# Half-swapped weight copies made on GpSimd in place of transfers, and a new order of the swap transfers

## The chip, the cores and the metric

The kernel runs on one core of a Trainium2 chip. Times are device microseconds of a whole execution, the median of several executions; the profile is one execution taken by the hardware profiler, and its span is some 2 us shorter than the time.

## The reference, cut to what matters

```python
# x: 2048 x 448;  H = 16 heads of 28;  F = 1792
q, k, v = split(x @ wqkv)
phi_q = concat(softmax(q @ w_phi), softmax(-(q @ w_phi)))     # per head
phi_k = concat(softmax(k @ w_phi), softmax(-(k @ w_phi)))
kv, z = phi_k^T @ v, sum over tokens of phi_k
a = (phi_q @ kv / (phi_q . z + 1e-6)) @ wo
b = gelu(x @ w1 + b1) @ w2 + b2
g = sigmoid((x * gate_w).sum(-1));   out = g * a + (1 - g) * b
```

## The kernel before: the parts that matter

The inner dimension 448 is 3.5 times 128. With x transposed in SBUF as `xT` (128 partitions, chunks 0 to 3, chunk 3 of use only in its upper 64 partitions), a plain product spends four matmuls on 3.5 chunks of work. The kernel therefore cuts 448 into seven pieces of 64 rows and lets the two 64-row halves of the array work at once, one for an even block of 512 tokens, one for the odd block after it. The array's lower half reads partitions 0 to 63 and its upper half 64 to 127, so each needs half of its pieces moved across by 64 partitions: `xS` holds those of x, `WqS`, `WkS`, `WvS` those of the weights.

```python
def x_half(i, k, h):                       # i: row half, k: piece 0..6, h: pair of blocks
    rows = slice(i * HP, (i + 1) * HP)     # HP = 64
    b = 2 * h + i
    if k == NK - 1:
        return xS[rows, 3, h, :] if i == 0 else xT[rows, 3, b * 512:(b + 1) * 512]
    if k % 2 == i:
        return xT[rows, k // 2, b * 512:(b + 1) * 512]
    return xS[rows, k // 2, h, :]

def swap_x(h):                             # ev, od: columns of the even and odd block of pair h
    nc.sync.dma_start(xS[0:HP, :, h, :], xT[HP:P, :, ev])          # "even half"
    nc.sync.dma_start(xS[HP:P, 0:3, h, :], xT[0:HP, 0:3, od])      # "odd half"

def load_x(b):                             # two transposing loads of block b from HBM
    nc.sync.dma_start_transpose(xT[:, 0:3, blk], x[blk, 0:384])    # "wide"
    nc.sync.dma_start_transpose(xT[:, 3, blk], x[blk, 320:448])    # "rest"

# ... earlier on the same queue: WkT, WqT, block 1
nc.gpsimd.dma_start(WvS[0:HP, 3, :], WvG[HP:P, 3, :])
nc.gpsimd.dma_start(x1o, xT[HP:P, 3, 512:1024])     # the "block 1 remainder"
load_x(2)
swap_w(WqS, Wpq)
swap_x(0)
load_x(3)
swap_w(WkS, Wpk)
swap_x(1)
swap_w(WvS, WvG, 3)
# ... w1, wo, w2

k_pair(0); k_pair(1); k_pair(2); k_pair(3)          # k of blocks 0 and 1: full-height matmuls
v_both()                                            # v of block 1: its last pieces paired, needs x1o, WvS
for g in range(4): q_pair(g, 0)                     # q of blocks 0, 1: needs xS pair 0, WqS
for r in range(4): k_two(r); v_two(r); q_pair(r, 1) # blocks 2, 3: need xS pair 1, WkS, WvS
# then 28 units of the dense layer, the kv sums, the output tiles
```

(The calls of `k_norm` between these, which normalize on VectorE and GpSimd, are cut.) All SyncE transfers go through one queue in this order.

The softmax here doesn't subtract the row's maximum and nothing guards it: scores larger than these inputs give would overflow.

## Time and profile before

| | before |
|---|---|
| time, median | 156.71 us (156.67 to 156.75) |
| span of the profiled execution | 154.7 us |
| TensorE busy | 149.5 us, 97% |
| its waits after the start | one, at 19.8 us, for `xS` |
| GpSimd busy | 34.1 us, 22% |
| DMA packets, bytes | 28306, 14.98 MB |

To read it: TensorE is nearly full, so what can be won is what it waits for; the DMA engines are full over the first third, and what they carry decides when TensorE may go on. The lines are in the prediction.

### The profile page before, as it was taken

Reading aid. Unit: us, or ns where it says so; the run is one execution under the profiler, and the core shown is the slowest. Engines: PE = TensorE matmul, PEld = TensorE weight load, DVE = VectorE, ACT = ScalarE, POOL = GpSimd, SP = SyncE. Lnnn points to the kernel's source line nnn. Section 1 sums busy time; section 2 is a strip of 40 time slices with the busy share of each in tenths; the row PEclk is TensorE's granted clock in tenths of the full one; section 3 lists DMA queues with packets and bytes.
Section 4 is the critical chain, followed back from the end, with each engine's and each line's share of the span. In section 5 each row is a group of like instructions: output and inputs, shape, how many; then the busy total and the mean of one; then the engine's idle time right before and its main releaser. Section 6 shows DMA issues by size and latency. Waiting matters only on the chain.

```text
span 154.7 us, 3189 instructions
## 1 busy us (share of the span) xinstructions
PE 149.5 (97%) x1302; PEld 81.2 (53%) x1302; DVE 83.1 (54%) x244; ACT 77.2 (50%) x93; POOL 34.1 (22%) x38
## 2 busy tenths in 40 slices
PE   7999979999999999999999999999999999999991
PEld 2775435555555854444444455555556555555561
DVE  3454989379892050000000059999977999977100
ACT  2569919999889626776767640111311111111121
POOL 7951596919876000000000000000000000000000
PEclk9999999999999999999999999999999999999999
DMA  4999999999993000000000001114332124338401
GB/s 150 229 232 154 209 233 254 221 222 215 218 356 130 4 0 4 0 0 4 0 0 0 4 0 34 34 38 96 92 96 64 40 64 92 82 82 39 121 31 30
DMA packets 28306, 14.98 MB, mean 97 GB/s; under 512 B 19938, under 2 KB 27876, under 8 KB 28292
## 3 DMA queue, kind: packets, MB, share of 16 engines
q1 hardware_dynamic: 27012, 14.00, 42.1%
q10 hardware_dynamic: 1152, 0.65, 1.5%
q0 software_dynamic: 128, 0.13, 0.7%
q8 instruction: 10, 0.16, 0.4%
q14 instruction: 4, 0.03, 0.1%
HBM read 6.11 MB, written 1.84 MB: 51 GB/s over the span
## 4 chain that ended last, share of the span: by engine, by line
PE 84%; SPq 9%; DMA 3%; issue 1%; DVE 0%; ACT 0%; ACTq 0%
PE hp L442 27%; PE y L501 27%; PE pq L320 8%; PE y L507 8%; PE nm L457 4%; PE v_ps L304 3%; PE pk L312 3%; DMA xS<-xT 3%; SPq L136 3%; PE acc L331 2%; SPq L132 2%; SPq L133 2%; SPq L384 1%; SPq L126 1%; SPq L141 0%
## 5 line engine op out<-in xcount | busy, mean ns | idle before, releaser
L501 PE MATMUL y<-w_sb,gel 128*128 128x448 bf16 (+2 forms) x238 | 45.2, 341 | 0.0
L442 PE MATMUL hp<-xT,w_sb 64*128 64x512 bf16 x196 | 42.3, 376 | 0.0
L442 PE MATMUL hp<-xS,w_sb 64*128 64x512 bf16 x196 | 41.9, 376 | 0.0
L447 ACT ACTIVATE gel<-hp,b1T 128x1024 bf16<-128x1024 f32 x28 | 30.8, 1110 | 13.0 <-PE hp L442 13.0
L510 ACT ACTIVATE res<-y,ungate 128x448 bf16<-128x448 f32 (+2 forms) x17 | 10.4, 611 | 50.3 <-PE y L507 50.2
L501 PEld LDWEIGHTS <-gel 128*128 128x128 bf16 x238 | 22.6, 98 | 19.6
L442 PEld LDWEIGHTS <-w_sb 64*128 64x128 bf16 x392 | 19.6, 94 | 22.5
L276 POOL TENSOR_TENSOR phik<-phik,rec 128x1792 bf16<-128x1792 bf16 (+1 forms) x8 | 24.9, 3126 | 9.8 <-DVE rec L273 9.8
L462 DVE COPY st<-nm 128x32 f32<-128x32 f32 x32 | 4.5, 184 | 35.5 <-PE nm L457 35.5
L478 DVE TENSOR_TENSOR tmp<-nm,al 128x448 bf16<-128x448 f32 x32 | 18.4, 617 | 0.0
L271 DVE TENSOR_REDUCE sums<-phik 128x64 f32<-128x1792 bf16 x8 | 16.0, 2000 | 2.8 <-ACT phik L264 2.8
L507 PE MATMUL y<-wo_sb,oT 128*128 128x448 bf16 (+2 forms) x68 | 14.7, 342 | 0.0
L320 PE MATMUL pq<-xT,Wpq 64*128 64x512 bf16 x56 | 13.0, 376 | 0.0
L320 PE MATMUL pq<-xS,WqS 64*128 64x512 bf16 x56 | 11.2, 376 | 0.9 <-DMA xS<-xT 0.9
L325 ACT ACTIVATE EqP<-pq 128x1024 bf16<-128x1024 f32 x8 | 8.4, 1051 | 5.1 <-PE pq L320 5.1
L193 DVE CAST vaug<-v_ps 128x896 bf16<-128x896 f32 x7 | 7.5, 1081 | 6.0 <-PE v_ps L304 3.3
L326 ACT ACTIVATE EqN<-pq 128x1024 bf16<-128x1024 f32 x8 | 8.4, 1055 | 0.0
L457 PE MATMUL nm<-KVbd,EqP 128*128 128x120 bf16 x64 | 8.3, 216 | 0.0
L457 PE MATMUL nm<-KVbd,EqN 128*128 128x120 bf16 x64 | 8.3, 216 | 0.0
L263 ACT ACTIVATE phik<-pk 128x896 bf16<-128x896 f32 x8 | 7.7, 961 | 0.3 <-PE pk L285 0.3
L507 PEld LDWEIGHTS <-oT 128*128 128x128 bf16 x68 | 6.0, 98 | 3.5
L264 ACT ACTIVATE phik<-pk 128x896 bf16<-128x896 f32 x8 | 7.8, 972 | 0.0
(99 smaller groups left out, 147.2 us busy)
## 6 DMA issues: line engine op xcount, KB each, us to landing
w_sb<-in_B_w_dram SPq DMA_DIRECT2D x4, 784.0 KB, 14.1
out_dram<-res SPq DMA_DIRECT2D x15, 112.0 KB, 1.9
w_sb<-in_B_w_dram SPq DMA_DIRECT2D x1, 1568.0 KB, 16.1
xS<-xT SPq DMA_DIRECT2D x2, 256.0 KB, 4.0
oT<-in_A_x_dram ACTq DMA_DIRECT2D x1, 448.0 KB, 3.2
xS<-xT SPq DMA_DIRECT2D x2, 192.0 KB, 4.3
WvS<-WvG SPq DMA_DIRECT2D x2, 168.4 KB, 3.9
wo_sb<-in_A_wo_dram SPq DMA_DIRECT2D x1, 336.0 KB, 17.1
```

The source lines that it names most:

```text
L271: nc.vector.reduce_sum(out=sums[:], in_=ph, axis=AX.X)
L276: eng.tensor_tensor(out=ph[:, lo:hi], in0=ph[:, lo:hi], in1=rec[:, lo:hi, :, None].to_broadcast([P, hi - lo, 2, DH]), op=ALU.mult)
L320: nc.tensor.matmul(pq[:, i, :], lhsT=w_half(Wpq, WqS, i, k)[:, g * P:(g + 1) * P], rhs=x_half(i, k, h), start=(k == 0), stop=(k == NK - 1))
L325: nc.scalar.activation(out=EqP[:, g, dst], in_=src, func=ACT.Exp)
L326: nc.scalar.activation(out=EqN[:, g, dst], in_=src, func=ACT.Exp, scale=-1.0)
L442: nc.tensor.matmul(hp[:, i, :], lhsT=w1_sb[i * HP:(i + 1) * HP, k, j * P:(j + 1) * P], rhs=x_half(i, k, h), start=(k == 0), stop=(k == NK ...
L447: nc.scalar.activation(out=gel[h][:, j, :], in_=hp[:].rearrange("p a b -> p (a b)"), func=ACT.Gelu_apprx_tanh, bias=b1T[:, j:j + 1])
L457: nc.tensor.matmul(nm[s][:, g * 2 * KW:(g + 1) * 2 * KW], lhsT=E[:, g, tok], rhs=KVbd[:, g, s, :], start=True, stop=True)
L478: nc.vector.tensor_tensor(out=tmp[:, s, :].rearrange("p (x h d) -> p x h d", x=NPR, h=2), in0=nmv[s][:, :, 0:PW].rearrange("p x (h d) -> p ...
L501: nc.tensor.matmul(y, lhsT=gel[t // 8][:, j, (t % 8) * P:(t % 8 + 1) * P], rhs=w2_sb[:, j, cols], start=(j == 0), stop=False)
L507: nc.tensor.matmul(y, lhsT=oT[:, c, tok], rhs=wo_sb[:, c, cols], start=False, stop=(c == NC4 - 1))
L510: nc.scalar.activation(out=res[:, cols], in_=y, func=ACT.Copy, scale=ungate[:, t:t + 1])
```

## The change

It has two parts. WkS, WvS and the block 1 remainder are made by GpSimd, which is almost idle between 9 and 17 us, by copies whose input and output are 64 partitions apart: 849 KB less for the DMA engines. And the first swap of x goes ahead of the loads of blocks 2 and 3.

```diff
-    nc.gpsimd.dma_start(WvS[0:HP, 3, :], WvG[HP:P, 3, :])
-    nc.gpsimd.dma_start(x1o, xT[HP:P, 3, 512:1024])
+    swap_on_pool(WvS, WvG)     # two nc.gpsimd.tensor_copy: [0:HP] <- [HP:P], [HP:P, 0:3] <- [0:HP, 0:3]
+    swap_on_pool(WkS, Wpk)
+    nc.gpsimd.tensor_copy(out=x1o, in_=xT[HP:P, 3, 512:1024])
+    swap_x(0, "even")
+    swap_w(WqS, Wpq)
+    swap_x(0, "odd")
     load_x(2)
-    swap_w(WqS, Wpq)
-    swap_x(0)
     load_x(3)
-    swap_w(WkS, Wpk)
     swap_x(1)
-    swap_w(WvS, WvG, 3)
```

The order of instructions on TensorE, VectorE and ScalarE stays as it was.

More of the change, by code (lines that the diff above doesn't have):

```diff
@@ L128, with load_x, swap_x @@
     nc.scalar.dma_start(wphi[:, 0:3, :], wphi_rows[0:384, :].rearrange("(c p) b -> p c b", p=P))
-    def load_x(b):
+    def load_x(b, part=None):
         blk = slice(b * 512, (b + 1) * 512)
-        nc.sync.dma_start_transpose(xT[:, 0:3, blk], x[blk, 0:384])
-        nc.sync.dma_start_transpose(xT[:, 3, blk], x[blk, 320:448])
+        if part != "rest":
+            nc.sync.dma_start_transpose(xT[:, 0:3, blk], x[blk, 0:384])
+        if part != "wide":
+            nc.sync.dma_start_transpose(xT[:, 3, blk], x[blk, 320:448])
     def load_wT(W, base):
         nc.sync.dma_start_transpose(W[:], A_wqkv[:, base:base + NC4 * P])
-    def swap_x(h):
+    def swap_x(h, part=None):
         ev = slice(2 * h * 512, 2 * h * 512 + 512)
         od = slice(2 * h * 512 + 512, 2 * h * 512 + 1024)
-        nc.sync.dma_start(xS[0:HP, :, h, :], xT[HP:P, :, ev])
-        nc.sync.dma_start(xS[HP:P, 0:3, h, :], xT[0:HP, 0:3, od])
+        if part != "odd":
+            nc.sync.dma_start(xS[0:HP, :, h, :], xT[HP:P, :, ev])
+        if part != "even":
+            nc.sync.dma_start(xS[HP:P, 0:3, h, :], xT[0:HP, 0:3, od])
     load_wT(WkT, D)
@@ L381, with swap_w, swap_on_pool @@
     prep(WqT, wq_at, (1, 0, 0))
-    def swap_w(W_S, W, chunks=NC4):
-        nc.sync.dma_start(W_S[0:HP, 0:chunks, :], W[HP:P, 0:chunks, :])
+    def swap_w(W_S, W):
+        nc.sync.dma_start(W_S[0:HP, :, :], W[HP:P, :, :])
         nc.sync.dma_start(W_S[HP:P, 0:3, :], W[0:HP, 0:3, :])
+    def swap_on_pool(W_S, W):
+        nc.gpsimd.tensor_copy(out=W_S[0:HP, :, :], in_=W[HP:P, :, :])
+        nc.gpsimd.tensor_copy(out=W_S[HP:P, 0:3, :], in_=W[0:HP, 0:3, :])
     nc.gpsimd.dma_start(b1c[0:NJ, :], B_b1.rearrange("(j p) -> j p", p=P))
     x1o = oT[0:HP, 1, 0:512]
-    nc.gpsimd.dma_start(WvS[0:HP, 3, :], WvG[HP:P, 3, :])
-    nc.gpsimd.dma_start(x1o, xT[HP:P, 3, 512:1024])
+    swap_on_pool(WvS, WvG)
[4 more added lines that the diff above has]
+    swap_x(0, "odd")
     load_x(2)
-    swap_w(WqS, Wpq)
-    swap_x(0)
     load_x(3)
-    swap_w(WkS, Wpk)
     swap_x(1)
-    swap_w(WvS, WvG, 3)
     for f in (slice(0, F // 2), slice(F // 2, F)):
```

## The prediction

> **What bounds the kernel now.** I read the page's busy table and slices first, to see which engine is full and where it is not.
>
> ```profile
> PE 149.5 (97%) x1302; PEld 81.2 (53%) x1302; DVE 83.1 (54%) x244; ACT 77.2 (50%) x93; POOL 34.1 (22%) x38
> ...
> PE   7999979999999999999999999999999999999991
> ...
> POOL 7951596919876000000000000000000000000000
> PEclk9999999999999999999999999999999999999999
> DMA  4999999999993000000000001114332124338401
> ```
>
> TensorE is busy for 97% of the 154.7 us span at full clock. One slice inside the run is not full: the sixth, 19.3 to 23.2 us. GpSimd (POOL) has a weak third slice (7.7 to 11.6 us) and an almost empty fourth (11.6 to 15.5 us), and the DMA engines are full from 4 us to about 46 us. So the question is what TensorE waits for in that slice. The waits of TensorE give it, the only wait of PE after its first instruction:
>
> ```profile
> PE pq L320 <- DMA xS<-xT: 0.9, 1, 0.9
> ```
>
> The timeline of TensorE (start, duration, line) shows it whole:
>
> ```profile
> 19.58 0.35 PE L220 MATMUL v_ps<-WvG,xT 64*128 64x449 bf16 x1
> 19.77 0.38 PE L320 MATMUL pq<-xT,Wpq 64*128 64x512 bf16 x1
> 21.03 0.39 PE L320 MATMUL pq<-xS,WqS 64*128 64x512 bf16 x2 [0.89 <-DMA xS<-xT]
> 21.24 0.39 PE L320 MATMUL pq<-xT,Wpq 64*128 64x512 bf16 x2
> ```
>
> The first query matmul of the lower 64 rows starts at 19.77. Its partner on the upper 64 rows would start 0.01 to 0.02 us later, as the pair at 19.57 and 19.58 did, but starts at 21.03: 1.24 us late. The 0.9 of the wait view is smaller because the earlier matmuls' modelled ends cover part. The chain that ended last says what it waits for and that nothing else follows:
>
> ```profile
> 16.40 4.59 DMA xS<-xT
> 20.99 0.04 issue
> 21.03 6.19 PE pq L320 x55
> 27.22 1.14 PE pk L312 x12
> ```
>
> From 21.03 to 151.5 us the chain is matmuls alone. So the change can give at most about 1.24 us here (one stagger of 0.2 us between the two row halves included), unless it breaks something else. The transfer in question is the second half of the swap of blocks 0 and 1 (L142), and the queue shows why it is late (start, duration of the issue):
>
> ```profile
> 8.97 1.26 SPq L133 DMA_TRANSPOSE xT<-in_A_x_dram  x1
> 10.27 1.71 SPq L132 DMA_TRANSPOSE xT<-in_A_x_dram  x1
> 12.03 1.26 SPq L133 DMA_TRANSPOSE xT<-in_A_x_dram  x1
> 13.47 0.56 SPq L383 DMA_DIRECT2D WqS<-Wpq  x1
> 14.08 1.52 SPq L384 DMA_DIRECT2D WqS<-Wpq  x1
> 15.64 0.65 SPq L141 DMA_DIRECT2D xS<-xT  x1
> 16.40 0.60 SPq L142 DMA_DIRECT2D xS<-xT  x1
> ```
>
> The transposes of block 2 (10.27 to 13.29), which nobody needs before the k matmuls at 26.87, stand ahead of it.
>
> **What the Trainium skill says.** "GPSIMD Engine Reference", section 4.1 (Engine selection), calls one-input operations on GpSimd roughly line-rate; section 3.1 puts light loops at 1.03 cycles an element and an ordinary tight loop at 1.8, at 1.2 GHz. The trace agrees with the first figure as far as it goes: the memset of 2048 elements took 1.80 us (0.88 ns each), the select rose from about 0.19 us for 4 elements to 0.29 us for 128 (0.8 ns each), and the two-input product of 1792 took 3.13 us (1.7 ns each, two reads). No large copy, and none between partitions, is in this trace. "SBUF — State Buffer", section "Who interferes with whom", says that VectorE instructions with two SBUF inputs, or in a 2-port mode, contend with GpSimd. The trace agrees: the half product at 46.32 us took 2.54 us instead of about 1.6 while VectorE ran the other half. Between 9.4 and 16.5 us VectorE does casts from fp32 PSUM (1.1 us for 896, one element a cycle) and a reduction, so I expect no such contention. "DMA: Bandwidth & Descriptors", section "Issuing engines are not separate DMA queues", says all queues share the same 16 engines; the trace agrees, DMA share 1.0 to 1.3 from 16 to 29 us at some 205 to 290 GB/s. So every byte taken out helps whatever stands behind it.
>
> **The change, part by part.**
> *Removed transfers.* WkS 224+168 KB, WvS 2x168.4 KB and 56 KB, x1o 64 KB: 849 KB. From the landing at 20.99 to that of the last xS transfer (issued 22.71, 4.0 to landing: 26.71), the queue moved block 3 (512 KB), WkS (392) and xS (448): 1352 KB in 5.72 us, 236 KB/us. So 849 KB is about 3.6 us of DMA time, of which WkS and x1o (456 KB, 1.9 us) lay ahead of that last landing.
> *The first swap.* The new queue is block 1, xS even, WqS, WqS, xS odd. xS even needs block 0 only, whose two PSUM copies end at 5.83 and 7.11, so it goes at 10.27. WqS waits for Wpq, whose casts end at 12.34 (VectorE) and 12.36 (ScalarE): 12.4 to 13.0 and 13.0 to 13.6 (up to 14.6, if the second takes 1.52 again). xS odd at 13.7 to 14.6, 1.8 to 2.7 us sooner; with 4.6 us to landing, 18.3 to 19.2, and with less ahead of it perhaps sooner. TensorE needs it at 19.79. The whole 1.24 us goes.
> *The copies on GpSimd.* 1796 + 1347 + 1792 + 1344 + 512 = 6791 elements in a row, five instructions. At 0.88 ns and 0.15 us each: 6.0 + 0.75 = 6.7 us. They start where the removed DMA started, 9.34; WvS is done about 12.4, WkS (its source is complete at 11.42) about 15.5, x1o about 16.1. TensorE wants x1o and WvS at 19.37 and WkS at 25.8. The first product on GpSimd started at 17.14. All hidden, with 3 us to spare for x1o; the limit is 10 us for 6791 elements, 1.37 ns each after the five fixed costs.
> *The later loads.* Block 2 is now issued at about 14.3 and block 3 at about 17.4 to 18.3 (before: 17.04), 3.1 us of issue each. The odd half of swap 1 waits for block 3's wide transpose: transposes took 3.8 to 5.7 us to landing, say 4.8, so 22.2 to 23.1 (before, its issue went at 22.71). With 2.2 to 3.5 us to landing, since WkS no longer stands ahead, it lands between 24.4 and 26.6; counting bytes alone, 26.71 - 1.9 = 24.8. TensorE arrives for it at 27.06 - 1.24 = 25.82. The gain is the smaller of 1.24 and 27.02 minus that landing: for 24.8, 1.24; for 26.0, 1.0; for 26.6, 0.4. I take 1.1.
> *Later.* w1 is issued some 2 us sooner than 25.03, and w2 after it; neither was waited for. ScalarE had idled 3.5 us ahead of its first query exponential (22.73), so it moves along with TensorE, as do the PSUM buffers it frees: the four buffers turn over with 0.8 us or more to spare.
> Sum: 156.71 - 1.1 = 155.6 us.
>
> **The rivals.**
> *The wait moves to the second swap.* For it: in the old trace xS odd landed at 26.71 for a use at 27.06, and WvS at 24.27 + 3.9 = 28.2 for 28.39, so this stage was already just in time, and block 3 now starts later if anything. Against it: 1.9 us of transfers ahead of it are gone, and WvS is off the queue. If it comes whole, the time is 156.3 to 156.7.
> *GpSimd becomes the bound.* For it: the skill's 1.8 cycles are 1.5 ns an element, 6791 x 1.5 = 10.2 + 0.75, x1o at 20.3, and TensorE waits 0.9 us at 19.37: 156.4 us. If crossing partitions cost 2.6 cycles (2.2 ns), x1o would come at 24.8 and the time be about 161. Against it: the memset and select slopes.
> *The gain is hidden.* If some other landing than xS odd (WqS, 14.08 + 4.9 = 19.0, close to the need) held the queries, less than 1.24 is won. Against it: WqS also moves about a microsecond up.
> *More is won.* TensorE waits nowhere else, so no.
>
> **Range and chances.** Some 60% for the full or nearly full gain (155.4 to 155.8), 25% for a part given back at the second swap, 10% for GpSimd late at x1o by about the same as is won, 4% for GpSimd slow enough to lose 2%. Hence 155.2 to 156.6. A gain of 2% is 3.1 us, more than all the waiting there is.
>
> **What would show it.** Right: no wait for xS at about 19.8; the first query exponential at about 21.5 rather than 22.73; five GpSimd copies of 1.3 to 1.7 us (0.6 the last) between 9.4 and 16.5; the end earlier by the same as the k matmuls. Wrong: a wait of the k matmuls at about 25.8 for xS (second swap late), of the v matmuls at 19.37 for GpSimd (copies slow), or casts of VectorE longer than 1.1 us between 9 and 16 (ports).

## The result, and the profile after

| | before | after |
|---|---|---|
| time, median of 4 | 156.69 us (156.59 to 156.75) | 155.45 us (155.35 to 155.66) |
| span of the profiled execution | 154.7 us | 153.4 us |
| DMA packets, bytes | 28306, 14.98 MB | 27922, 14.11 MB |

The ratio is 0.9923, 95% interval 0.9906 to 0.9941. Ratios here are the mean time of one kernel's runs over that of the other's runs of the same rounds, so not quite the ratio of the medians quoted. The change is faster by 0.8%, 1.24 us in the medians.

Three rows of slices from the page of the changed kernel, and the only wait of PE that its trace shows, the one at the start:

```profile
PE   7999999999999999999999999999999999999992
...
POOL 7999796949874000000000000000000000000000
...
DMA  4996998999990000000000001124332123334411
```

```profile
PE warm_ps L371 <- DVE w_sb L115: 1.1, 1, 1.1
```

The weak sixth slice of PE is full now, and GpSimd's third and fourth slices hold the copies. The DMA row shows room in the fourth slice (11.5 to 15.3 us) and a little in the seventh (23.0 to 26.8 us), where it was full before. The timeline of TensorE around the old wait:

```profile
19.81 0.35 PE L224 MATMUL v_ps<-WvG,xT 64*128 64x449 bf16 x1
20.00 0.38 PE L324 MATMUL pq<-xT,Wpq 64*128 64x512 bf16 x1
20.00 0.59 PE L324 MATMUL pq<-xS,WqS 64*128 64x512 bf16 x2
```

The partner on the upper rows starts with the first matmul, at 20.00, not 1.24 us after it. (In this execution everything from 6 us on is 0.23 us later than in the profile of before, because TensorE waited that long for a load of WvG, at 6.2 us; the old profile had v matmuls at 19.57 where this one has 19.81.) The queue and GpSimd:

```profile
10.57 0.73 SPq L144 DMA_DIRECT2D xS<-xT  x1
12.76 0.50 SPq L387 DMA_DIRECT2D WqS<-Wpq  x1
13.32 1.49 SPq L388 DMA_DIRECT2D WqS<-Wpq  x1
14.90 0.62 SPq L146 DMA_DIRECT2D xS<-xT  x1
15.57 1.73 SPq L133 DMA_TRANSPOSE xT<-in_A_x_dram  x1
...
21.59 0.62 SPq L144 DMA_DIRECT2D xS<-xT  x1
23.10 0.59 SPq L146 DMA_DIRECT2D xS<-xT  x1
```

```profile
9.59 1.68 POOL L391 COPY WvS<-WvG 64x1796 bf16<-64x1796 bf16 x1
11.31 1.31 POOL L392 COPY WvS<-WvG 64x1347 bf16<-64x1347 bf16 x1
12.66 1.68 POOL L391 COPY WkS<-Wpk 64x1792 bf16<-64x1792 bf16 x1
14.38 1.30 POOL L392 COPY WkS<-Wpk 64x1344 bf16<-64x1344 bf16 x1
15.74 0.61 POOL L398 COPY oT<-xT 64x512 bf16<-64x512 bf16 x1
17.39 6.38 POOL L280 TENSOR_TENSOR phik<-phik,rec 128x1792 bf16<-128x1792 bf16 x2 [1.03 <-DVE rec L277]
```

The odd half of the first swap went at 14.90 and landed 3.1 us later, at 18.0, two microseconds ahead of its use. The odd half of the second went at 23.10, after a gap: the even half's issue ended at 22.21, and the queue then waited 0.9 us for block 3's wide load. It landed 2.8 us later, at 25.9, as the view of the transfers issued from 22.5 to 23.6 us has it (KB, us to landing):

```profile
xS<-xT SPq DMA_DIRECT2D x1, 192.0 KB, 2.8
```

These are the loads of the first weights for the k matmuls of blocks 2 and 3 (PEld), and the first two of those matmuls:

```profile
25.83 0.09 PEld L316 LDWEIGHTS <-xT 64*128 64x128 bf16 x1
25.93 0.21 PEld L316 LDWEIGHTS <-xS 64*128 64x128 bf16 x2
...
26.04 0.35 PE L316 MATMUL pk<-Wpk,xT 64*128 64x448 bf16 x1
26.05 0.54 PE L316 MATMUL pk<-WkS,xS 64*128 64x448 bf16 x2
```

The weights from xS are loaded 0.10 us after those of the other row half, as the swap lands, and still the two matmuls start together. So the second swap arrives just as it is needed: no wait shows, and there is about a tenth to spare. GpSimd is done at 16.35, with 1.03 us idle before its next product and 3.3 us before TensorE needs the remainder at 19.61.

### The profile page after: what moved, and what is told of

Same layout as the page of the kernel before. It is cut to its first block, busy times and chain, and to the rows that moved or that the text cites. A ratio compares the mean times of both kernels' runs of the same rounds, so it can differ in the third digit from the quotient of the medians.

```text
span 153.4 us, 3189 instructions
## 1 busy us (share of the span) xinstructions
PE 149.4 (97%) x1302; PEld 79.8 (52%) x1302; DVE 83.0 (54%) x244; ACT 77.3 (50%) x93; POOL 39.8 (26%) x41
## 2 busy tenths in 40 slices
DMA packets 27922, 14.11 MB, mean 92 GB/s; under 512 B 19842, under 2 KB 27780, under 8 KB 27908
## 4 chain that ended last, share of the span: by engine, by line
PE 97%; ACT 0%; issue 0%; DVE 0%; ACTq 0%
PE y L509 28%; PE hp L450 28%; PE y L515 8%; PE pq L324 8%; PE nm L465 4%; PE pk L289 4%; PE v_ps L308 3%; PE pk L316 3%; PE acc L335 2%; PE v_ps L209 2%; PE warm_ps L371 2%; PE v_ps L219 2%; PE w_ps L236 1%; PE xp L354 1%; PE v_ps L222 0%; ACT res L518 0%
## 5 line engine op out<-in xcount | busy, mean ns | idle before, releaser
L450 PE MATMUL hp<-xS,w_sb 64*128 64x512 bf16 x196 | 42.6, 376 | 0.0
L450 PEld LDWEIGHTS <-w_sb 64*128 64x128 bf16 x392 | 19.0, 94 | 23.0
L324 PE MATMUL pq<-xS,WqS 64*128 64x512 bf16 x56 | 12.9, 376 | 0.0
```

Source lines behind the costliest of these rows:

```text
L324: nc.tensor.matmul(pq[:, i, :], lhsT=w_half(Wpq, WqS, i, k)[:, g * P:(g + 1) * P], rhs=x_half(i, k, h), start=(k == 0), stop=(k == NK - 1))
L450: nc.tensor.matmul(hp[:, i, :], lhsT=w1_sb[i * HP:(i + 1) * HP, k, j * P:(j + 1) * P], rhs=x_half(i, k, h), start=(k == 0), stop=(k == NK ...
```

## The experiments

The theory after the result: TensorE alone sets the end, the change removed the one wait that it had (1.24 us), the new order did that, and the copies keep that wait from coming back at the second swap. The rivals: the order alone does it; the copies alone do it by relieving the DMA engines; the copies are near a limit of their own. Twelve kernels were run, five rounds each besides the profile, six executions in all; they ran in three groups, each on a chip of its own with its own executions of the kernel before, whose medians were 156.63, 156.68 and 156.79 us. So runs of different groups are compared by their ratios. (One group is order alone, copies alone and the two with more on GpSimd; another is WkS and WvS as transfers, wide loads first and the first run with paired k; the third is the rest.) All were correct.

| run | median, us (range) | ratio to before, 95% interval | wait of TensorE in its profile |
|---|---|---|---|
| changed, again | 155.51 (155.32 to 155.63) | 0.9920 (0.9902 to 0.9939) | none for a swap |
| order alone | 157.25 (156.75 to 157.57) | 1.0045 (1.0025 to 1.0066) | second swap |
| copies alone | 156.26 (155.88 to 156.58) | 0.9983 (0.9964 to 1.0002) | first swap |
| changed, WkS as transfers | 156.72 (156.65 to 157.19) | 1.0006 (0.9983 to 1.0030) | second swap |
| the same, from GpSimd's queue | 156.51 (156.13 to 156.88) | 0.9986 (0.9965 to 1.0006) | second swap |
| changed, WvS as transfers | 155.19 (154.99 to 155.65) | 0.9904 (0.9881 to 0.9927) | none for a swap |
| order, WkS copy alone | 155.37 (154.99 to 155.49) | 0.9910 (0.9891 to 0.9929) | none |
| 3 us more on GpSimd | 155.50 (155.22 to 156.05) | 0.9940 (0.9918 to 0.9962) | none |
| 6 us more on GpSimd | 158.60 (158.53 to 160.16) | 1.0164 (1.0127 to 1.0202) | for GpSimd |
| wide loads first | 155.40 (155.27 to 155.46) | 0.9912 (0.9892 to 0.9933) | none |
| that, paired k of block 1 | 155.38 (155.10 to 155.68) | 0.9914 (0.9890 to 0.9938) | none for a swap |
| that, gate row later | 157.12 (155.93 to 157.66) | 1.0015 (0.9982 to 1.0049) | for x's first block |

### Each part alone

The order alone:

```diff
-    swap_on_pool(WvS, WvG)
-    swap_on_pool(WkS, Wpk)
-    nc.gpsimd.tensor_copy(out=x1o, in_=xT[HP:P, 3, 512:1024])
+    nc.gpsimd.dma_start(WvS[0:HP, 3, :], WvG[HP:P, 3, :])
+    nc.gpsimd.dma_start(x1o, xT[HP:P, 3, 512:1024])
     ...
     load_x(3)
+    swap_w(WkS, Wpk)
     swap_x(1)
+    swap_w(WvS, WvG, 3)
```

> The new queue order alone; WkS, WvS and the block 1 remainder stay transfers. Theory (order removes the first wait, and the copies keep the second swap from becoming the new wait): no wait for xS at about 19.8, but WkS's 392 KB stand ahead of the second swap again, 392/236 = 1.7 us, so TensorE waits some 1.2 to 1.8 us at the first k matmuls of blocks 2 and 3 (about 25.8): 156.6 to 157.2 us. Rival (the order is the whole gain, the copies only tidy up): no wait, 155.45 us.

It took 157.25 us, slower than before the change and 0.05 us over the expected range. TensorE's waits and timeline in it:

```profile
PE pk L316 <- DMA xS<-xT: 1.1, 1, 1.1
...
27.67 0.36 PE L316 MATMUL pk<-WkS,xS 64*128 64x448 bf16 x2 [1.14 <-DMA xS<-xT]
```

The first wait is gone and a larger one stands at the k matmuls of blocks 2 and 3, which start at 27.67 instead of 26.05; the v matmuls then start their second row half 0.29 us after the first (29.11 against 28.82), as the second transfer of WvS lands (issued at 25.16, 3.9 us to landing). The first rival falls: the order alone gives back more than it wins.

The copies alone (the kernel after, with `load_x(2)`, `swap_w(WqS)`, `swap_x(0)`, `load_x(3)`, `swap_x(1)` in the old order):

> The GpSimd copies alone, queue order as before (block 2's transposes ahead of the first swap). Theory: the first wait stays, less at most 0.3 us for the 64 KB of the block 1 remainder: xS lands at 20.7 to 21.0, 156.4 to 156.7 us, and the second swap lands well ahead of its use. Rival (the bytes taken off the DMA engines make the gain): the first wait is gone, 155.45 us.

156.26 us, ratio 0.9983: a tenth or two under the expected range, but the ratio is the 0.3 us that the theory allowed. The chain shows the old wait in its old place:

```profile
16.32 4.55 DMA xS<-xT
20.91 6.19 PE pq L324 x55
```

So the parts do not add: +0.45% for the one and -0.17% for the other, where both together gave -0.8%.

### Which of the copies is needed

WkS put back as transfers, the rest as changed:

```diff
-    swap_on_pool(WkS, Wpk)
     ...
     load_x(3)
+    swap_w(WkS, Wpk)
     swap_x(1)
```

> The changed kernel with WkS alone put back as two transfers between block 3's transposes and the second swap. Theory (the second swap lands in the changed kernel just as it is needed, near 25.9): 392 KB more ahead of it, 1.2 us of issue and up to 1.7 us of transfer; TensorE waits 0.7 to 1.7 us at the first k matmuls of blocks 2 and 3: 156.1 to 157.1 us. Rival (its landing was not the limit, there is slack): 155.45 us.

156.72 us, the time of before: the whole gain went. Its queue and TensorE:

```profile
21.56 0.59 SPq L387 DMA_DIRECT2D WkS<-Wpk  x1
...
23.62 0.62 SPq L146 DMA_DIRECT2D xS<-xT  x1
...
28.00 0.36 PE L316 MATMUL pk<-WkS,xS 64*128 64x448 bf16 x2 [1.36 <-DMA xS<-xT]
```

The odd half is issued only 0.5 us later than in the changed kernel (23.62 against 23.10), since the queue had to wait for block 3's load there anyway, but takes 4.3 us to land instead of 2.8. The profiled execution is one of the two slower of the six (157.16 us), so its wait is some tenths longer than the usual one.

WvS put back, behind the second swap (`swap_w(WvS, WvG, 3)` after `swap_x(1)`, its chunk 3 still copied by GpSimd):

> The changed kernel with WvS put back as two transfers of 168 KB behind the second swap; its chunk 3 for the v matmuls of block 1 stays a GpSimd copy. Theory: they land at 25.9 + 337/236 = 27.3 or a little later, the first use is at 27.37: 155.4 to 156.0 us, so that WvS is worth little of the gain, at most 0.5 us. Rival (all 849 KB count alike): 156.4 us or more.

155.19 us, 0.2 under the expected range: nothing lost. Its interval overlaps those of the changed kernel, so I call neither faster. Then the smallest version, order and WkS copy, with WvS and the block 1 remainder transferred as before the change:

> The smallest version: new queue order and WkS on GpSimd; WvS and the block 1 remainder stay transfers as before the change (WvS behind the second swap). Theory (WkS's copy is all that the order needs): 155.2 to 155.7 us, the same as the changed kernel. Rival (the other copies carry a part): 156 us or more.

155.37 us. Of the 849 KB taken off the queue, only the 392 KB of WkS counted. They stood ahead of the second swap; so did 64 KB of the remainder and 56 KB of WvS (its chunk 3), and this run puts those back without a loss that it could show.

### Is it their bytes or their place?

WkS as transfers once more, but issued by GpSimd at 12.50, in place of its two copies:

```diff
-    swap_on_pool(WkS, Wpk)
+    nc.gpsimd.dma_start(WkS[0:HP, :, :], Wpk[HP:P, :, :])
+    nc.gpsimd.dma_start(WkS[HP:P, 0:3, :], Wpk[0:HP, 0:3, :])
```

> The changed kernel with WkS as two transfers again, but issued by GpSimd at about 12.6 us, in the place of its two copies. Theory (what the WkS transfers cost in the run that put them back is their place ahead of the second swap; the DMA engines have idle time between 14 and 21 us): no wait at the k matmuls of blocks 2 and 3; at most some tenths at the first swap, since the 392 KB now share the engines with WqS and xS: 155.4 to 156.0 us. Rival (the bytes themselves are what counts, wherever they are issued): 156.5 us or more, as with the transfers in the other queue.

156.51 us, the rival's number: my theory of the place fell. The SyncE queue shows where the time went (compare the same lines of the changed kernel above):

```profile
14.23 1.68 SPq L146 DMA_DIRECT2D xS<-xT  x1
15.96 2.54 SPq L133 DMA_TRANSPOSE xT<-in_A_x_dram  x1
...
24.21 0.59 SPq L146 DMA_DIRECT2D xS<-xT  x1
```

The first swap's odd half landed in time (5.3 us after its issue instead of 3.1), but the issues behind it were drawn out, block 3's wide load went at 19.84 instead of 18.65, and the second swap's odd half at 24.21 instead of 23.10; TensorE started on it at 27.03. The work is the same 392 KB, in another queue and nine microseconds earlier, and 1.0 us is lost. Why the issues took longer is not shown. The mean busy share of the DMA engines from 12 to 18 us in the changed kernel is 0.80, and 0.90 in this run; I had read that as room, and it was not room that costs nothing. A later issue from GpSimd's queue, behind block 3's loads, was not tried.

### How far GpSimd is from a limit

Two more copies ahead of the block 1 remainder, each within the partitions that it reads:

```diff
+    spare = oT[:, 2, 0:1796].rearrange("p (c d) -> p c d", c=NC4)
+    nc.gpsimd.tensor_copy(out=spare[HP:P], in_=WvG[HP:P, :, :])
+    nc.gpsimd.tensor_copy(out=spare[:, 0:3, :], in_=WvG[:, 0:3, :])
     nc.gpsimd.tensor_copy(out=x1o, in_=xT[HP:P, 3, 512:1024])
```

> The changed kernel with two more GpSimd copies ahead of the block 1 remainder, one of 1796 elements on 64 partitions and one of 1347 on 128, both into the partitions that they read. Theory (GpSimd had over 3 us to spare): the remainder ends at 16.35 + 3.0 = 19.35, need 19.6, no wait, 155.45 us; and if crossing partitions and the number of partitions cost nothing, they take 1.68 and 1.31 us as the crossing ones did. Rival (the copies are already at the edge or disturb VectorE): 156 us or more; if crossing costs, the new copies are faster than 1.6 and 1.25 us.

155.50 us, no wait. Its GpSimd timeline:

```profile
15.57 1.68 POOL L399 COPY oT<-WvG 64x1796 bf16<-64x1796 bf16 x1
17.32 1.31 POOL L400 COPY oT<-WvG 128x1347 bf16<-128x1347 bf16 x1
```

These copies cross no partitions, and the second uses all 128; they take 1.68 and 1.31 us, the same as the crossing ones on 64. So crossing by 64 partitions costs nothing here, nor does the number of partitions (128 against 64).

All four half swaps done twice (6 us more):

> The changed kernel with all four half swaps of WvS and WkS on GpSimd done twice, 6.0 us more ahead of the block 1 remainder. Theory: it ends at 16.35 + 6.0 = 22.3, TensorE wants it at 19.6, waits 2.7 us, 158.1 us (157.8 to 158.4). Rival (v matmuls can slide, or something else hides it): under 157 us.

158.60 us; four executions within 0.1 us of it, two at 160.1. The profile has the wait as expected:

```profile
PE v_ps L222 <- POOL oT L400: 2.7, 1, 2.7
```

The time is 0.2 us above the expected range: the four copies took 6.20 us with the gaps between them, not 6.0, and the matmul that waits starts at 22.59, 2.98 us later than in the changed kernel (the wait view says 2.7 because the modelled ends of the matmuls before cover part). The two slower executions had a granted clock of 0.989, the others 1.0; with so few nothing more can be said. So GpSimd becomes the bound between 3 and 6 us of extra work, as the dates say.

### Does the changed kernel lose anything at the second swap, and is there a faster one?

The second swap lands with a tenth to spare in the one profile, so other executions might lose some tenths there. The changed kernel with `load_x(2, "wide")`, `load_x(3, "wide")`, then both rests, then the odd half of swap 1 ahead of the even:

> The changed kernel with the wide transposes of blocks 2 and 3 ahead of both remainders, and the odd half of the second swap ahead of the even. Theory (TensorE waits for nothing any more): the odd half lands near 24.6 instead of 25.9, with no gain: 155.3 to 155.5 us. Rival (runs of the changed kernel lose some tenths at the second swap that the one profile does not show): 155.1 us or less.

155.40 us, against 155.51 for the changed kernel repeated:

> The changed kernel unaltered, for a comparison on one chip with the three runs beside it: 155.3 to 155.6 us, ratio 0.992.

The two ran in different groups; their ratios, 0.9912 and 0.9920, differ by some 0.13 us, and each interval is some 0.3 us wide to either side. So no gain is shown, and a loss of a few tenths is not excluded by the times. The profiles show none: with the wide loads first the weights from xS are loaded at 25.75 together with those of the other row half, and the two k matmuls start at 25.96; in the repeat of the changed kernel the loads are 0.08 us apart (25.77 and 25.85), and both matmuls start at 25.98.

A faster version, tried twice. With the first half of WkS and the remainder there by 14.8 us (the remainder's copy goes ahead of WkS's second one for this), the k matmuls of block 1 can pair their last 64 rows as its v matmuls do, two slots of 0.19 us fewer:

```diff
-    k_pair(2)
     k_norm(1)
-    k_pair(3, b1=True)
+    k_both()       # 12 full-height matmuls, then 4 half-height ones in pairs, with WkS[0:HP, 3] and x1o
     v_both()
```

> An attempt at a faster version: as the run with the wide transposes first, and the k matmuls of block 1 done as its v matmuls are: the last 64 rows of two tiles in the two row halves at once, from the GpSimd copies of WkS and of the block 1 remainder, which are there by about 15.1. Two slots of 0.19 us fewer on TensorE: 155.45 - 0.38 = 155.07 us (154.9 to 155.3). Rival (the copies come too late for it at about 16.7, or ScalarE's exponentials, started later, hold the queries): 155.4 us or more.

155.38 us: no gain shown. The profile says where it went: from the first k matmul to the first v matmul took 5.91 us (11.22 to 17.13) instead of 6.12 (11.01 to 17.13, wide loads first), so 0.21 us was won, not 0.38. Twelve full-height matmuls took 2.37 us to the first half-height one where 12 x 0.189 = 2.27 was due, and the way back took 0.28 instead of 0.19. "TensorEngine Tiling (Array Packing)", section "Key Properties", in the Trainium skill says that a change of tiling mode drains the engine; the two tenths agree with it. And in the profiled execution the 0.21 us was lost again ahead of it, where the weight products waited for WqT's load, from 10.06 (9.78 + 0.28 of steady work, estimated from the four matmuls before) to 10.28.

So I tried to bring WqT sooner, with the small gate row, whose wait for a memset holds the queue until 1.27 us, behind the first load of WvG:

> Second attempt at a faster version: the paired k matmuls of block 1 as before, and the small gate transfer, whose wait for a memset held the whole queue to 1.27 us, behind the first WvG transfer, so that Wq's transposed load lands some 0.4 us sooner and no longer holds the weight products at about 10. Expected: the 0.2 us that the paired k matmuls saved in the profile and 0.1 to 0.3 of waits at the start: 154.9 to 155.3 us. Rival (x's first block, sharing the engines with an earlier WvG, lands later by as much): 155.4 us.

157.12 us, a miss. The rival was right in kind, but where it named 155.4 us, 1.7 us were lost:

```profile
PE xp L374 <- DMA oT<-in_A_x_dram: 1.3, 1, 1.3
```

x's first block, 448 KB on the other queue, now shares the engines with an earlier WvG load; it took 4.7 us to land instead of 3.2, and TensorE's first transposes start at 5.55 instead of 4.05 us. One of the six executions took 155.93 us, so the delay does not come every time. In this run, what starts first at the head of the kernel mattered more than the 0.4 us of queue. No version beat the changed kernel by more than the intervals.

## Why the prediction was right

**What bounds the kernel, and the ceiling.** Right: the wait for the odd half of the first swap was worth 1.24 us and all else of TensorE was without gaps. That the medians differ by exactly 1.24 us is luck in the second decimal: between the two profiled executions TensorE's last matmuls move up by 1.02 us (from 151.26 to 150.24), 1.24 won and 0.23 lost at the start, and the interval of the ratio allows 0.9 to 1.5 us.

**The first swap.** Right in kind; its dates were off. The even half went at 10.57, WqS at 12.76 and 13.32 (the second took 1.49 again, though block 2 no longer stood ahead of it), the odd half at 14.90, 0.3 us after the latest date given; but it landed in 3.1 us, not 4.6, at 18.0, earlier than the 18.3 to 19.2 predicted. In the repeat's profile these four went at 10.36, 12.70, 13.26 and 14.66, so a tenth or two of the lateness is that of one execution.

**The copies.** Right: 6.58 us of copies against 6.7, done at 16.35 against 16.1; no cast of VectorE grew (1.09 and 0.61 us between 9.3 and 11.0, as before). The 3 us to spare for the remainder held, as the runs with 3 and 6 us more show. The page "GPSIMD Engine Reference", section 4.1, with its "roughly line-rate" for one input was the one to go by, not the 1.8 cycles of section 3.1 (the page's best case for a tight loop unrolled four times, and a pessimistic choice for a copy here): (1.68 - 0.61) / (1796 - 512) is 0.83 ns an element, one cycle at the page's 1.2 GHz.

**The later loads.** The step that was loosest. The odd half of the second swap went at 23.10, at the late end of 22.2 to 23.1, and landed at 25.9, inside 24.4 to 26.6. The count of bytes (24.8) did not decide: block 3's wide load did. By the prediction's own formula 25.9 is a gain of 1.1. In this execution TensorE, late by 0.23 us from the start, came to these matmuls at 26.04, so the landing cost it nothing: they start 1.01 us earlier than before (26.05 against 27.06). The estimate of 1.1 for the gain was 0.14 us under what was measured.

**The removed transfers.** 849 KB was right, but the sum hides that WvS and the remainder were worth nothing. The 392 KB at 236 KB/us, 1.66 us, is of the right size: in the run that put WkS back the k matmuls started at 28.00, 1.70 us after the 26.30 at which the partner would have started. That profile is of a slow one of its six executions; the medians differ by 1.2 to 1.3 us.

**The rivals.** The wait at the second swap did not come, but it was the near miss: it is what every run with the new order and without the WkS copy shows. GpSimd as the bound did not come, and its 2.6 cycles for crossing partitions were a supposition that the copies refute (1.0 cycle by the slope above). The third, WqS landing late, did not show: it landed 3.6 us after 13.32, at 16.9.

**Readings that were off, none of which carried the result.** The 3.13 us for the product of 1792 is a mean that mixes two shapes; that product took 3.21 us, 1.8 ns an element, and the one of 896 took 2.54. The DMA share from 16 to 29 us was 0.93 to 1.29, and from 16 to 17.2 us the GpSimd queue had 1.7% of it against 105.5% for SyncE's, so those figures do not show queues sharing the engines; the run with WkS in GpSimd's queue is the better evidence. w1 went at 23.74, 1.3 us sooner and not 2, without consequence.

## What to carry to other kernels

When one queue feeds an engine that is nearly full, list for each transfer when it lands and when it is wanted: a reorder that brings one forward pushes the rest back, and here it lost time until the right 392 KB left the DMA engines. A copy between partitions that GpSimd has idle time for can take such bytes off, and only those ahead of the next tight landing count. Moving the same transfer to another queue, earlier, did not help here.

## What the Trainium skill lacked or had wrong

- "GPSIMD Engine Reference" has no figure for a plain copy. Here bf16 copies took 1.68 us for 1796 elements a partition, 1.31 for 1347 and 0.61 for 512, the same on 64 and on 128 partitions, and the same within partitions as 64 partitions across, which no page that I read prices.
- "DMA: Bandwidth & Descriptors", section "Issuing engines are not separate DMA queues", is borne out (WkS from GpSimd's queue: 156.51 us against 155.51 with copies), but gives nothing for how time to landing grows with what is in flight: the odd halves of the swaps, 192 KB each, took 2.8, 3.1, 4.3 and 5.3 us to landing in these runs.
- "TensorEngine Tiling (Array Packing)", section "Key Properties", says that a change of mode drains TensorE, without a cost: about 0.1 us each way here (2.37 us against 2.27 into the half-height matmuls, 0.28 against 0.19 out of them).
